# Score bursts of three pieces that run on from batch to batch, in an attention and squared-ReLU kernel

## The chip, the cores and the metric

The kernel runs on one core of one Trainium2 chip. A core has five engines, each with a queue of its own that is worked through in order: TensorE (PE) multiplies matrices into the eight banks of PSUM, VectorE (DVE) and ScalarE (ACT) move and transform data, GpSimd (POOL) does casts here, and SyncE (SP) issues most of the DMA transfers. Instructions wait for each other through semaphores. The metric is the device time of one execution in microseconds, lower is better. The kernel before takes 339.43 us, the median of three runs (338.14 to 339.49).

## The reference

Eight batches of eight heads, 576 tokens, 64 channels per head; 16 beacon keys and values stand ahead of the 576 ordinary ones and are seen by every token. The attention output becomes 4608 rows of 512 channels, which go through a two-layer network with a squared ReLU.

```python
k_all = np.concatenate([beacon_k, k], axis=2)          # (8, 8, 592, 64)
v_all = np.concatenate([beacon_v, v], axis=2)
scores = scale * np.matmul(q, k_all.transpose(0, 1, 3, 2))
scores = np.where(causal, -1e9, scores)                # causal for the 576 keys
a = np.exp(scores - scores.max(-1, keepdims=True))
a /= a.sum(-1, keepdims=True) + 1e-09
x = np.matmul(a, v_all)                                # then to (4608, 512)
h = x @ w_in                                           # (512, 2048)
out = np.square(np.maximum(h, 0)) @ w_out              # (2048, 512)
```

## The kernel before, in words

**Attention.** A batch `b` has four head pairs; pair `p = 4 * b + pr`. Queries and keys are held transposed (`qT`, `kT`: channels of the two heads on partitions 0-63 and 64-127), keys in five blocks of 128. Only the block pairs on or below the diagonal are computed. For batches 1 to 7 the scores of a pair are cut into four *pieces* (`WHOLE`, pieces 0 to 3): three pieces with 512 columns per head, and a fourth with 128 columns (keys of block 0, queries 368 to 496). A piece takes a pair of PSUM banks, one for each head; ScalarE's `exp` (line 781) moves it to its offset in the pair's buffer `pt` (four of these). In the kernel before, the fourth pieces of pairs 0 and 1 share one pair of banks, and those of pairs 2 and 3 another (`SHARED`), each still with an `exp` of its own into its own `pt`. So a batch has 14 bank pairs of scores and 16 `exp`.

**Bursts.** The score matmuls (line 764) use half of the array's rows for each head, the two heads at once; the planner calls this mode "rows", all other matmuls are "full". Scores are issued in *bursts*: one planned operation `qk<pair>.0.<first piece>` computes two or three bank pairs back to back (`SIZES`). From batch 2 on a batch is five bursts of 3, 3, 3, 3 and 2 bank pairs.

**After a pair's four exps** VectorE masks the diagonal (lines 799, 803, `mask`), TensorE multiplies by the values (line 819, `av`: 30 matmuls with `pt` as the weights), and VectorE divides by the sum (lines 834, 835, `norm`) into `xn`. When all four pairs of a batch are normalized, five DMA transposes `xt<b>.0` to `xt<b>.4` (line 866, issued by SyncE, one for each 128-token tile of the batch) put the batch into `xT`, channels on partitions. Batch 0 does this on TensorE instead.

**The network.** The 4608 tokens are worked in nine chunks of 512 (`chunk j`). A chunk has 16 groups `s1.<j>.<f>` of four matmuls (line 947: `xT` by `w_in`), whose results ACT or DVE move with a ReLU (lines 964, 966) and DVE squares (line 973), then 32 blocks of matmuls `s2` (line 987: by `w_out`), whose results ACT copies out (line 437) and SyncE stores, two stores `st<j>.0` and `st<j>.1` for a chunk (line 1012). A chunk begins when its tokens are in `xT`: chunk 3 (tokens 1536 to 2047) needs `xt3.0` to `xt3.2` of batch 3 (which begins at token 1728), chunk 4 (2048 to 2559) needs `xt4.0` to `xt4.2`. Chunk 4 wraps around the ring that `xT` is, so each of its groups is two times four matmuls of 256 columns, and only the second four read batch 4.

**Loads.** `ld<b>k<c>`, `ld<b>q<c>`, `ld<b>v<c>` bring 128 rows of keys, queries or values each into one of eight staging buffers `stg` (lines 483, 484; 256 KB for 128 rows, and a small one of the beacon rows ahead of block 0), GpSimd casts them to bf16 (line 439). From batch 3 on queries and keys are transposed by one large DMA each, `tr<b>q` and `tr<b>k` (line 516), out of `qk_area`. From batch 2 on all of these, the `xt` and the `st` are issued by SyncE, one queue in order.

**What sets the order.** Nothing is scheduled at run time: `Order.run` plans the whole program once, with a duration for each operation, pools for the PSUM banks and buffers, and a list of free engines. On each engine it starts, of the operations whose dependencies, buffers and gate are satisfied in its plan, the one with the lowest `prio`. The order so found is what each engine's queue contains; on the chip the engines follow it, each waiting where data are not there. A burst's `prio` is 100 times its first pair plus the number of its first piece.

Of the kernel before, what the change touches and what calls it, by code (L numbers as in the profile page):

```python
# [129 lines left out]
class Order:  # L130
# [180 lines left out]
def kernel(  # L311
# [11 lines left out]
    nc = tc.nc  # L323
# [17 lines left out]
    def sb(name, shape, dt):  # L341
        return pool.tile(shape, dt, name=name)
# [16 lines left out]
          for i in range(2)]  # L359
    ks = [qk_area[0:NP, (2 * i + 1) * WS:(2 * i + 2) * WS].rearrange("p (h s d) -> p h s d", h=H, s=NS)  # L360
          for i in range(2)]
    bks = sb("bks", [128, H, D], BF16)
    spare = {x: sb(f"spare{x}", [NP, NS * 2 * D], BF16) for x in "kq"}
    vb = [sb(f"vb{i}", [128, NT, H, D + 1], BF16) for i in range(2)]
# [13 lines left out]
    def pair(op, k=0):  # L378
        return ps[:, op.held[k]:op.held[k] + 2, :]
# [4 lines left out]
    def act(n):  # L384
        return 0.066 + n / 1200.0
# [6 lines left out]
    def wait_for(later, first):  # L392
# [1 line left out]
            mybir.DependencyClass.Sync, mybir.DependencyReason.DATA), reason="order of loads")  # L394

    order = Order(
        pools={"ps": Banks(), "stg": Slots(NSTG), "pt": Slots(NPT)},
        limits={"late": 4, "strip": 6, "av": 4, "mlp": 4, "tp": 6},
        floors={"mlp": 2},
        keep=2,  # L400
# [266 lines left out]
    class Phase:  # L667
# [3 lines left out]
        def __init__(self, pieces, diag, last, tiles, off):  # L671
# [30 lines left out]
    ONE_BY_ONE = [[(x, i)] for x in range(HP) for i in range(4)]  # L702
    SHARED = [[(0, 0)], [(0, 1)], [(0, 2)], [(0, 3), (1, 3)], [(1, 0)], [(1, 1)], [(1, 2)], [(2, 0)], [(2, 1)],
              [(2, 2)], [(2, 3), (3, 3)], [(3, 0)], [(3, 1)], [(3, 2)]]
    PIECES = {b: ONE_BY_ONE if b < 1 else SHARED for b in range(B)}
    SIZES = {b: [2] * 7 if b < 2 else [3, 3, 3, 3, 2] for b in range(B)}

    def phases(b):
        return SPLIT if b < NSPLIT else WHOLE
# [26 lines left out]
    def add_scores(pairs, n, sizes, pieces):  # L736

        work = []
        for shared in pieces:
            at, parts = 0, []  # L740
            for x, i in shared:
                parts.append((pairs[x], i, at, phases(pairs[x].b)[n].pieces[i]))
                at += parts[-1][3][2]
            work.append(parts)
        exps = {x.p: [] for x in pairs}
        at = 0
        for size in sizes:
            group = work[at:at + size]
            at += size
            lead = group[0][0][0]  # L750
            prio = 100.0 * lead.p + 1000.0 * n + group[0][0][1]
            every = [part for parts in group for part in parts]
            cols = sum(t1 - t0 for _, _, _, (mms, _, _) in every for _, t0, t1, _ in mms)
            owners = list({x.p: x for x, _, _, _ in every}.values())
            box = {}

            def emit_qk(e, group=group, box=box):
                for k, parts in enumerate(group):
                    st = pair(box["qk"], k)
                    for x, _, lo, (mms, _, _) in parts:  # L760
                        for c, t0, t1, col in mms:
                            for hj in range(2):
                                hp = slice(64 * hj, 64 * hj + 64)
                                nc.tensor.matmul(  # L764
                                    st[:, hj, lo + col:lo + col + t1 - t0],
                                    kT[x.b % 2][hp, x.pr, 128 * c:128 * c + 128],
                                    qT[x.b % 2][hp, x.pr, t0:t1],
                                    start=True, stop=True,
                                )

            qk = add(f"qk{lead.p}.{n}.{group[0][0][1]}", "PE", cols / 2400.0, emit_qk, prio=prio,
                     deps=[d for x in owners for d in x.qk_deps + [x.take_pt]],
                     take=("ps", "late" if lead.b < NSPLIT and n else "strip", [2] * size), gate=lead.gate, mode="rows")
            box["qk"] = qk
            for x in owners:
                qk_ops[x.p].append(qk)
            for k, parts in enumerate(group):
                own = []
                for x, i, lo, (_, off, width) in parts:
                    def emit_exp(e, off=off, width=width, k=k, x=x, lo=lo, box=box):  # L780
                        nc.scalar.activation(pt[x.take_pt.held[0]][:, :, off:off + width],  # L781
                                             pair(box["qk"], k)[:, :, lo:lo + width], AF.Exp, bias=0.0, scale=scale)

                    own.append(add(f"exp{x.p}.{n}.{i}", "ACT", act(2 * width), emit_exp, prio=prio + 0.1 * k,
                                   deps=[qk], give=(qk, k) if len(parts) == 1 else None))
                    exps[x.p].append(own[-1])
                if len(parts) > 1:
                    add(f"share{lead.p}.{n}.{k}", "-", 0.0, None, deps=own, give=(qk, k))
        assert at == len(work)
        for x in pairs:  # L790
            add_phase(x.b, x.pr, x.p, n, phases(x.b)[n], x.take_pt, exps[x.p])

    def add_phase(b, pr, p, n, ph, take_pt, exps):
# [12 lines left out]
        mask = add(f"mask{p}.{n}", "DVE", 0.08 + 0.15 * ph.diag[3] + (0.26 if ph.last else 0.0), emit_mask,  # L806
                   prio=base, deps=exps + [tri_op])
        tl, nt = ph.tiles, len(ph.tiles)

        def emit_av(e):  # L810
            P = pt[take_pt.held[0]]
            a = pair(av)
            for hj in range(2):
                h = 2 * pr + hj
                for t in tl:
                    for c in range(t + 1):
                        rr = rows_of(c)
                        o = ph.off[c, t]
                        nc.tensor.matmul(  # L819
                            a[:, hj, (t - tl[0]) * (D + 1):(t - tl[0] + 1) * (D + 1)],  # L820
                            P[0:rr, hj, o:o + 128],
                            vb[b % 2][0:rr, c, h, :],
                            start=(c == 0), stop=(c == t),
                        )
# [236 lines left out]
    for b in range(B):  # L1061
# [26 lines left out]
        if b < NSPLIT:  # L1088
            for x in pairs:
                for n, ph in enumerate(phases(b)):  # L1090
                    add_scores([x], n, [1] * len(ph.pieces), [[(0, i)] for i in range(len(ph.pieces))])
        else:
            add_scores(pairs, 0, SIZES[b], PIECES[b])
        if b < NXPE:
            add_xt_pe(b)
        else:
            add_xt(b)
        for j in range(NCH):
            if min(((j + 1) * TCH - 1) // S, B - 1) == b:
                late.append(j)  # L1100
        if b >= 1:
            for j in late:
                add_chunk(j)
            late = []

    turns = TURNS.split()
    named = {o.name: o for o in order.ops}
# [35 lines left out]
```

## Time and profile before

| | us |
|---|---|
| median of three runs | 339.43 |
| lowest and highest | 338.14, 339.49 |
| the profiled execution, its own time | 338.65 |
| its span, first to last instruction | 336.9 |
| PE busy in the span | 327.1 |
| ACT busy | 193.6 |
| DVE busy | 160.5 |
| POOL busy | 86.8 |

The profile has a page and views that are asked of the trace. Busy time counts matmuls, weight loads (PEld), vector and scalar operations and casts; DMA-issuing instructions stand under SPq. A row of the *chain of waits* gives start, length and what the chain ran through: TensorE's matmuls of one line, until another line follows. A row of the *timeline* gives start, length, engine, line and operation; for SPq the length is the time that the issuing instruction held the queue. A row of a *line's view* gives shortest, median and longest duration, first and last start, and the time from issue to landing for DMAs. A row of the *windows* gives each engine's busy time in a stretch, the granted TensorE clock, the busy share of the 16 DMA engines and what they moved.

### The profile page before, as it was taken

Reading aid. Unit: us, or ns where it says so; the run is one execution under the profiler, and the core shown is the slowest. Engines: PE = TensorE matmul, PEld = TensorE weight load, DVE = VectorE, ACT = ScalarE, POOL = GpSimd, SP = SyncE. Lnnn points to the kernel's source line nnn. Section 1 sums busy time; section 2 is a strip of 40 time slices with the busy share of each in tenths; the row PEclk is TensorE's granted clock in tenths of the full one; section 3 lists DMA queues with packets and bytes.
Section 4 is the critical chain, followed back from the end, with each engine's and each line's share of the span. In section 5 each row is a group of like instructions: output and inputs, shape, how many; then the busy total and the mean of one; then the engine's idle time right before and its main releaser. Section 6 shows DMA issues by size and latency. Waiting matters only on the chain.

```text
span 336.9 us, 7692 instructions
## 1 busy us (share of the span) xinstructions
PE 327.1 (97%) x3172; PEld 184.2 (55%) x3172; DVE 160.5 (48%) x323; ACT 193.6 (57%) x300; POOL 86.8 (26%) x135
## 2 busy tenths in 40 slices
PE   3999999999999999999999999999999999999995
PEld 2778766545545555554468845545554544444444
DVE  6669977267604761475245632673246503301400
ACT  3887974597457647465656745755656226515611
POOL 7765911425122605140512351220000000000000
PEclk9999999999999999999999999999999999999999
DMA  9999999699959999799989996991310041011003
GB/s 167 196 207 210 206 203 207 147 247 179 221 104 223 241 199 176 185 208 228 206 121 257 242 210 138 209 196 32 104 62 2 14 120 63 0 62 64 0 17 110
DMA packets 138211, 50.38 MB, mean 150 GB/s; under 512 B 124176, under 2 KB 133264, under 8 KB 138176
## 3 DMA queue, kind: packets, MB, share of 16 engines
q1 hardware_dynamic: 128304, 40.42, 57.7%
q0 software_dynamic: 9520, 9.11, 16.3%
q8 instruction: 25, 0.41, 0.6%
q10 hardware_dynamic: 352, 0.36, 0.4%
q14 instruction: 10, 0.08, 0.1%
HBM read 37.22 MB, written 9.44 MB: 138 GB/s over the span
## 4 chain that ended last, share of the span: by engine, by line
PE 93%; DMA 2%; POOL 1%; DVE 1%; issue 1%; ACT 0%; POOLq 0%
PE ps L947 37%; PE ps L987 36%; PE ps L819 9%; PE ps L764 8%; DMA qk_area<-in_q_dram 2%; PE ps L635 1%; PE ps L1030 1%; POOL qk_area L599 1%; PE ps L883 1%; DVE g L966 0%; PE ps L537 0%; POOL vb L439 0%; PE ps L533 0%; POOL w_in L908 0%; DVE g L973 0%
## 5 line engine op out<-in xcount | busy, mean ns | idle before, releaser
L947 PE MATMUL ps<-xT,w_in 128*128 128x512 bf16 (+3 forms) x704 | 133.7, 340 | 0.2
L987 PE MATMUL ps<-w_out,g 128*128 128x512 bf16 x560 | 128.4, 379 | 0.0
L781 ACT ACTIVATE pt<-ps 128x1024 bf16<-128x1024 f32 (+3 forms) x128 | 102.9, 874 | 18.3 <-PE ps L764 18.1
L947 PEld LDWEIGHTS <-w_in 128*128 128x128 bf16 x704 | 65.9, 98 | 55.2 <-issue 3.9
L964 ACT ACTIVATE g<-ps 128x512 bf16<-128x512 f32 (+2 forms) x116 | 65.5, 568 | 39.1 <-PE ps L947 38.6
L987 PEld LDWEIGHTS <-g 128*128 128x128 bf16 x560 | 52.1, 98 | 61.1 <-issue 3.6
L973 DVE TENSOR_TENSOR g<-g 128x1024 bf16<-128x1024 bf16 (+2 forms) x80 | 52.1, 654 | 69.6 <-ACT g L964 69.4
L437 ACT COPY osb<-ps 128x512 f32<-128x512 f32 (+2 forms) x37 | 21.3, 576 | 68.8 <-PE ps L987 54.6
L439 POOL CAST qk_area<-stg 128x512 bf16<-128x512 f32 (+2 forms) x50 | 34.2, 688 | 67.5 <-DMA stg<-in_q_dram 41.0
L439 POOL CAST vb<-stg 128x512 bf16<-128x512 f32 (+1 forms) x39 | 26.1, 675 | 63.3 <-DMA stg<-in_v_dram 63.2
L799 DVE TENSOR_TENSOR pt<-pt,tri 128x1024 bf16<-128x1024 bf16 (+1 forms) x36 | 23.5, 654 | 34.2 <-ACT pt L781 34.2
L819 PEld LDWEIGHTS <-pt 128*128 128x128 bf16 (+1 forms) x960 | 34.2, 98 | 6.3 <-ACT pt L781 0.4
L966 DVE TENSOR_SCALAR g<-ps 128x512 bf16<-128x512 f32 (+2 forms) x44 | 26.8, 611 | 19.7 <-PE ps L947 19.4
L819 PE MATMUL ps<-vb,pt 128*128 128x65 bf16 (+1 forms) x960 | 35.6, 195 | 0.4 <-POOL vb L439 0.3
L764 PE MATMUL ps<-qT,kT 64*128 64x80 bf16 (+6 forms) x680 | 32.9, 235 | 0.0
L764 PEld LDWEIGHTS <-kT 64*128 64x128 bf16 x680 | 19.0, 96 | 16.8 <-issue 13.8
L835 DVE TENSOR_TENSOR xn<-ps,rcp 128x640 bf16<-128x640 f32 (+2 forms) x36 | 27.0, 750 | 1.8 <-DVE rcp L834 0.5
L834 DVE RECIPROCAL rcp<-ps 128x10 f32<-128x10 f32 (+2 forms) x36 | 7.5, 209 | 28.9 <-PE ps L819 28.9
L437 ACT COPY qT<-ps 128x576 bf16<-128x576 bf16 x12 | 7.6, 644 | 8.4 <-PE ps L635 7.4
L803 DVE TENSOR_TENSOR pt<-pt,tri 80x160 bf16<-80x160 bf16 x32 | 11.1, 347 | 0.0
L439 DVE COPY kT<-ps 128x576 bf16<-128x576 bf16 x12 | 8.9, 751 | 1.8 <-PE ps L638 1.2
L635 PE MATMUL ps<-ident,sparek 96*128 96x96 bf16 x18 | 1.5, 229 | 5.8 <-DVE sparek L439 5.8
(52 smaller groups left out, 80.4 us busy)
## 6 DMA issues: line engine op xcount, KB each, us to landing
out_dram<-osb SPq DMA_DIRECT2D x17, 512.0 KB, 3.6
stg<-in_v_dram SPq DMA_DIRECT2D x20, 256.0 KB, 5.1
stg<-in_q_dram SPq DMA_DIRECT2D x20, 256.0 KB, 5.5
stg<-in_k_dram SPq DMA_DIRECT2D x15, 256.0 KB, 4.3
w_in<-in_moe_w_in_dram POOLq DMA_DIRECT2D x4, 512.0 KB, 8.8
w_out<-in_moe_w_out_dram POOLq DMA_DIRECT2D x4, 512.0 KB, 11.6
stg<-in_v_dram SPq DMA_DIRECT2D x7, 224.0 KB, 4.5
qk_area<-in_k_dram POOLq DMA_DIRECT2D x4, 288.0 KB, 11.5
```

The lines of the kernel that those rows point to most:

```text
L437: nc.scalar.copy(dst, src)
L439: eng[e].tensor_copy(dst, src)
L764: nc.tensor.matmul(st[:, hj, lo + col:lo + col + t1 - t0], kT[x.b % 2][hp, x.pr, 128 * c:128 * c + 128], qT[x.b % 2][hp, x.pr, t0:t1], sta ...
L781: nc.scalar.activation(pt[x.take_pt.held[0]][:, :, off:off + width], pair(box["qk"], k)[:, :, lo:lo + width], AF.Exp, bias=0.0, scale=scale)
L799: nc.vector.tensor_tensor(out=d, in0=d, in1=tri[:, m0:m0 + m, :][:, None].to_broadcast([128, 2, m, 128]), op=ALU.min)
L819: nc.tensor.matmul(a[:, hj, (t - tl[0]) * (D + 1):(t - tl[0] + 1) * (D + 1)], P[0:rr, hj, o:o + 128], vb[b % 2][0:rr, c, h, :], start=(c = ...
L835: nc.vector.tensor_tensor(out=xn[b % 2].rearrange("p t (h d) -> p h t d", d=D)[:, 2 * pr:2 * pr + 2, tl[0]:tl[0] + nt], in0=a[:, :, :, 0:D ...
L947: nc.tensor.matmul(h[:, lo - spans[0][0]:hi - spans[0][0]], w_in_sb[:, mc, ft * 128:(ft + 1) * 128], xT[:, mc, lo % RING:lo % RING + hi - lo],
L964: nc.scalar.activation(dst, h, AF.Relu, bias=0.0, scale=1.0)
L966: nc.vector.tensor_scalar(out=dst, in0=h, scalar1=0.0, scalar2=None, op0=ALU.max)
L973: nc.vector.tensor_tensor(out=d, in0=d, in1=d, op=ALU.mult)
L987: nc.tensor.matmul(o, G[:, fc, ts * 128:(ts + 1) * 128], w_out_sb[:, fc, :], start=(fc == 0), stop=(fc == NFT - 1))
```

## The change

For batches 3 to 7 (`FLOW = 3`) the fourth pieces of all four pairs go into one bank pair, 128 columns for each pair, with one `exp` (`expr<b>`) that moves the 1024 columns to a place of its own, `rest` (two buffers, in the part of `qk_area` that the keys of batch 1 used), from which `av` takes the weights for that block. A batch then has 13 bank pairs and 13 `exp`. These form a list, `flow`: the fourth pieces first, then pieces 0, 1, 2 of each pair. Bursts take three from the head of the list, and what is left of a batch waits for the next batch and is issued in one burst with its first pieces; only after batch 7 is a shorter burst made (two). The operations after the scores are added to the plan when a pair's pieces have all been put into bursts. Batches 0 to 2 are unchanged.

```diff
+    rest = [qk_area[:, 4 * W + 1024 * i:4 * W + 1024 * (i + 1)].rearrange("p (h w) -> p h w", h=2) for i in range(2)]
...
-        pools={"ps": Banks(), "stg": Slots(NSTG), "pt": Slots(NPT)},
+        pools={"ps": Banks(), "stg": Slots(NSTG), "pt": Slots(NPT), "rest": Slots(2)},
...
-    PIECES = {b: ONE_BY_ONE if b < 1 else SHARED for b in range(B)}
-    SIZES = {b: [2] * 7 if b < 2 else [3, 3, 3, 3, 2] for b in range(B)}
+    PIECES = {0: ONE_BY_ONE, 1: SHARED, 2: SHARED}
+    SIZES = {0: [2] * 7, 1: [2] * 7, 2: [3, 3, 3, 3, 2]}
+    FLOW = 3
...
+        slots = [x.take_pt for x, _, _, (_, off, _) in every if off is not None] + [
+            x.take_rest for x, _, _, (_, off, _) in every if off is None]
...
+            if parts[0][3][1] is None:
+                x = parts[0][0]
+
+                def emit_rest(e, k=k, x=x, box=box):
+                    nc.scalar.activation(rest[x.take_rest.held[0]], pair(box["qk"], k), AF.Exp, bias=0.0, scale=scale)
+
+                o = add(f"expr{x.b}", "ACT", act(2 * 512), emit_rest, prio=prio + 0.1 * k, deps=[qk], give=(qk, k))
+                for x, _, _, _ in parts:
+                    exps[x.p].append(o)
+                continue
...
+    def add_flow(pairs, last):
...
+        pieces = WHOLE[0].pieces
+        (c, t0, t1, _), = pieces[3][0]
+        flow.append([(x, 3, 128 * n, ([(c, t0, t1, 0)], None, 128)) for n, x in enumerate(pairs)])
+        flow.extend([(x, i, 0, pieces[i])] for x in pairs for i in range(3))
+        done = []
+        while len(flow) >= 3 or (last and flow):
+            group = [flow.pop(0) for _ in range(min(3, len(flow)))]
+            add_burst(group, 0, flow_exps)
+            for parts in group:
+                for x, _, _, _ in parts:
+                    flow_left[x.p] -= 1
+                    if not flow_left[x.p]:
+                        add_phase(x.b, x.pr, x.p, 0, phases(x.b)[0], x.take_pt, flow_exps[x.p], x)
+                        if x.pr == HP - 1:
+                            add(f"restg{x.b}", "-", 0.0, None, deps=[o for i in range(HP) for o in av_ops[HP * x.b + i]],
+                                give=x.take_rest)
+                            done.append(x.b)
+        return done
...
                         o = ph.off[c, t]
+                        keys = P[0:rr, hj, o:o + 128]
+                        if x is not None and (c, t) == (0, 3):
+                            keys = rest[x.take_rest.held[0]][:, hj, 128 * pr:128 * pr + 128]
...
-        else:
+        elif b < FLOW:
             add_scores(pairs, 0, SIZES[b], PIECES[b])
...
+        for bb in add_flow(pairs, b == B - 1) if b >= FLOW else [b]:
+            if bb < NXPE:
+                add_xt_pe(bb)
+            else:
+                add_xt(bb)
```

The bodies of the bursts moved from `add_scores` into `add_burst` are otherwise as before.

More of the change, by code (lines that the diff above doesn't have):

```diff
@@ L747, in add_scores @@
         for size in sizes:
-            group = work[at:at + size]
+            add_burst(work[at:at + size], n, exps)
             at += size
[L750 to L788, printed above, removed]
@@ L791, in add_scores, with add_burst, emit_qk, emit_exp @@
             add_phase(x.b, x.pr, x.p, n, phases(x.b)[n], x.take_pt, exps[x.p])
-    def add_phase(b, pr, p, n, ph, take_pt, exps):
+    def add_burst(group, n, exps):
+        lead = group[0][0][0]
+        prio = 100.0 * lead.p + 1000.0 * n + group[0][0][1]
+        every = [part for parts in group for part in parts]
+        cols = sum(t1 - t0 for _, _, _, (mms, _, _) in every for _, t0, t1, _ in mms)
+        owners = list({x.p: x for x, _, _, _ in every}.values())
+        slots = [x.take_pt for x, _, _, (_, off, _) in every if off is not None] + [
+            x.take_rest for x, _, _, (_, off, _) in every if off is None]
+        box = {}
+        def emit_qk(e, group=group, box=box):
+            for k, parts in enumerate(group):
+                st = pair(box["qk"], k)
+                for x, _, lo, (mms, _, _) in parts:
+                    for c, t0, t1, col in mms:
+                        for hj in range(2):
+                            hp = slice(64 * hj, 64 * hj + 64)
+                            nc.tensor.matmul(
+                                st[:, hj, lo + col:lo + col + t1 - t0],
+                                kT[x.b % 2][hp, x.pr, 128 * c:128 * c + 128],
+                                qT[x.b % 2][hp, x.pr, t0:t1],
+                                start=True, stop=True,
+                            )
+        qk = add(f"qk{lead.p}.{n}.{group[0][0][1]}", "PE", cols / 2400.0, emit_qk, prio=prio,
+                 deps=[d for x in owners for d in x.qk_deps] + list({id(o): o for o in slots}.values()),
+                 take=("ps", "late" if lead.b < NSPLIT and n else "strip", [2] * len(group)), gate=lead.gate, mode="rows")
+        box["qk"] = qk
+        for x in owners:
+            qk_ops[x.p].append(qk)
+        for k, parts in enumerate(group):
+            own = []
+            if parts[0][3][1] is None:
[6 more added lines that the diff above has]
+                continue
+            for x, i, lo, (_, off, width) in parts:
+                def emit_exp(e, off=off, width=width, k=k, x=x, lo=lo, box=box):
+                    nc.scalar.activation(pt[x.take_pt.held[0]][:, :, off:off + width],
+                                         pair(box["qk"], k)[:, :, lo:lo + width], AF.Exp, bias=0.0, scale=scale)
+                own.append(add(f"exp{x.p}.{n}.{i}", "ACT", act(2 * width), emit_exp, prio=prio + 0.1 * k,
+                               deps=[qk], give=(qk, k) if len(parts) == 1 else None))
+                exps[x.p].append(own[-1])
+            if len(parts) > 1:
+                add(f"share{lead.p}.{n}.{k}", "-", 0.0, None, deps=own, give=(qk, k))
@@ new lines @@
+    flow, flow_exps, flow_left, whole = [], {}, {}, []
+    def add_flow(pairs, last):
+        b = pairs[0].b
+        take_rest = add(f"rest{b}", "-", 0.0, None, prio=100.0 * pairs[0].p, deps=pairs[0].qk_deps, take=("rest", "rest", [1]),
+                        gate=pairs[0].gate)
+        for x in pairs:
+            x.take_rest = take_rest
+            flow_exps[x.p] = []
+            flow_left[x.p] = 4
+        pieces = WHOLE[0].pieces
[16 more added lines that the diff above has]
+        return done
@@ L794, in add_phase @@
+    def add_phase(b, pr, p, n, ph, take_pt, exps, x=None):
         base = 100.0 * p + 1000.0 * n
@@ L818, in emit_av @@
                         o = ph.off[c, t]
+                        keys = P[0:rr, hj, o:o + 128]
+                        if x is not None and (c, t) == (0, 3):
+                            keys = rest[x.take_rest.held[0]][:, hj, 128 * pr:128 * pr + 128]
                         nc.tensor.matmul(
                             a[:, hj, (t - tl[0]) * (D + 1):(t - tl[0] + 1) * (D + 1)],
-                            P[0:rr, hj, o:o + 128],
+                            keys,
                             vb[b % 2][0:rr, c, h, :],
@@ L1091 @@
                     add_scores([x], n, [1] * len(ph.pieces), [[(0, i)] for i in range(len(ph.pieces))])
-        else:
+        elif b < FLOW:
             add_scores(pairs, 0, SIZES[b], PIECES[b])
[L1094 to L1104, printed above, removed]
+        for bb in add_flow(pairs, b == B - 1) if b >= FLOW else [b]:
[3 more added lines that the diff above has]
+                add_xt(bb)
+            for j in range(NCH):
+                if min(((j + 1) * TCH - 1) // S, B - 1) == bb:
+                    late.append(j)
+            if bb >= 1:
+                for j in late:
+                    add_chunk(j)
+                late = []
     turns = TURNS.split()
```

## The prediction

> **What bounds the kernel now.** I read the page's busy shares first, then the windows, to see where the busiest engine has gaps, then the chain of waits.
>
> ```profile
> PE 327.1 (97%) x3172; PEld 184.2 (55%) x3172; DVE 160.5 (48%) x323; ACT 193.6 (57%) x300; POOL 86.8 (26%) x135
> ```
>
> ```profile
> 0.00:66.25 66.25, 59.78 (x837) 42.88 (x838) 47.95 (x131) 44.51 (x74) 36.78 (x61) 1.00 1.08 192
> 66.25:333.54 267.29, 267.28 (x2336) 141.32 (x2336) 112.30 (x191) 148.82 (x226) 50.05 (x74) 1.00 0.68 140
> 333.54:336.90 3.36, 0.00 (x0) 0.00 (x0) 0.29 (x1) 0.27 (x1) 0.00 (x0) 1.00 0.27 88
> ```
>
> In a row of the windows the first number after the stretch is its length, the second TensorE's busy time, and the last three are the granted clock, the DMA share and GB/s. From 66.25 to 333.54 us TensorE has no gap: 267.28 of 267.29 us, at clock 1.00. The idle time lies ahead of that, in a part the change does not touch. So two things alone can move the time: work taken off TensorE counts in full, and so does each new wait of TensorE, since its queue is in order and nothing behind a waiting matmul can pass it.
>
> **What the change takes away: three bursts.** What a burst costs beside its columns is read from the chain of waits.
>
> ```profile
> 160.18 1.73 PE ps L987 x8
> 161.91 0.77 PE ps L764 x20
> 162.68 3.56 PE ps L987 x16
> 166.24 0.67 PE ps L764 x20
> 166.91 1.83 PE ps L987 x8
> ...
> 224.10 0.54 PE ps L764 x8
> ...
> 232.58 0.77 PE ps L764 x20
> ```
>
> Eight `s2` matmuls of 512 columns take 1.73 us after a value burst, so 0.216 each or 0.422 ns a column, and 1.83 us right after a score burst: leaving a burst costs 0.10. The bursts of 0.77, 0.67 and 0.54 us have 1536, 1280 and 1024 columns for each of two heads that run at once; at 0.422 ns that is 0.65, 0.54 and 0.43, so entering costs 0.11 to 0.13. I take 0.2 us for a burst in all. Five batches had 25 bursts; five times 13 bank pairs in threes are 21 bursts and one of two, 22. Columns and matmuls stay the same in number. Gain: 3 x 0.2 = 0.6 us. A bound from the other side is the time that the weight loader stood idle:
>
> ```profile
> PEld L764 <- issue: 13.8, 37, 0.4
> ...
> PEld L987 <- issue: 3.6, 17, 0.2
> ```
>
> 13.8 over 37 entries is 0.37 and 3.6 over 17 exits is 0.21; if all of it were lost array time, a burst would cost 0.58 and the gain be 1.7 us. The straight line through the three lengths (0.23 us for 512 columns leaves 0.08 at none) gives 0.18 a burst, 0.5 us. I take 0.6, because the lengths of whole matmul runs are closer to what the end sees than the idle time of a loader that runs ahead.
>
> **What it changes off the path.** A batch loses four exps of 256 elements and gets one of 1024:
>
> ```profile
> L781 ACT ACTIVATE pt<-ps 128x1024 bf16<-128x1024 f32 x84 | 82.7, 1034 | 8.3 <-PE ps L764 8.3
> ...
> L781 ACT ACTIVATE pt<-ps 128x256 bf16<-128x256 f32 x28 | 9.5, 395 | 8.5 <-PE ps L764 8.5
> ```
>
> 4 x 0.395 - 1.034 = 0.55 us less for ScalarE in each batch, 2.7 in all. ScalarE is 57% busy and its idle time costs nothing, so I count 0; between 0 and the 2.7 us gain that would follow if TensorE waited for it, the window without a gap says 0. If that cover went, by an exp that came late, TensorE would wait about one exp, 1.03 us. The value matmuls load the same 128x128 weights from `rest` instead of `pt`: no change. In batches 3 and 6 the burst that begins with the fourth pieces is planned behind the one that begins with the first pair's piece 2 (its number, 3, is the higher), which delays `av12` by one burst, with other work in between.
>
> **What it moves: the DMA transposes behind loads.** The two programs' orders, which are fixed when they are built, differ on two queues. On TensorE a batch's last pair is finished later, since its last piece waits for the next batch: of batch 3, `av15` now comes after four runs of eight `s2` matmuls of chunk 2 rather than after one. Behind it the planner has put more of SyncE's loads ahead of the transposes that feed the network. Ahead of `xt3.0` now stand in addition `ld5q3`, `ld5k1`, `ld5q4`, `ld5k2` and the store `st2.0`; ahead of `xt4.0` in addition `ld6q4`, `ld6k2`, `ld6k3`, `ld6k4` and `ld6v0`. The matmuls that read these transposes keep about their place on TensorE. So the question is what room the transposes have.
>
> ```profile
> 126.18 3.51 SPq L484 DMA_DIRECT2D stg<-in_q_dram  x3
> 129.79 7.72 SPq L866 DMA_TRANSPOSE xT<-xn  x5
> ...
> 137.60 0.53 SPq L484 DMA_DIRECT2D stg<-in_q_dram  x1
> 138.23 0.53 SPq L484 DMA_DIRECT2D stg<-in_k_dram  x1
> 138.85 0.95 SPq L1012 DMA_DIRECT2D out_dram<-osb  x1
> 139.89 0.65 SPq L484 DMA_DIRECT2D stg<-in_q_dram  x1
> 140.64 0.86 SPq L484 DMA_DIRECT2D stg<-in_k_dram  x1
> ```
>
> ```profile
> L866 SPq DMA_TRANSPOSE xT<-xn x2: 1260/1616/1973, 131.6 to 133.6; - x2
> ...
> DMA to landing us min/median/max: 2.6/3.3/4.1
> ```
>
> ```profile
> L866 SPq DMA_TRANSPOSE xT<-xn x2: 1257/1257/1257, 167.3 to 168.6; - x2
> ...
> DMA to landing us min/median/max: 2.6/3.4/4.2
> ```
>
> The first fence is SyncE's queue: the five rows after the transposes are just the five instructions that now go ahead of them. The other two hold `xt3.1` and `xt3.2`, and `xt4.1` and `xt4.2`: of the first two, the second (issued at 133.6) landed 2.6 us later, at 136.2; of the others, the second (168.6) took 4.2 and landed at 172.8. When are they wanted?
>
> ```profile
> 138.74 0.86 PE ps L947 x4
> ...
> 173.99 0.87 PE ps L947 x8
> ```
>
> Those are the first groups of chunks 3 and 4: the transposes had 2.5 and 1.6 us to spare (chunk 4 reads batch 4 only with its second four matmuls, at 174.4). In the changed order, ahead of chunk 3 stand one `s2` run of eight more (+1.73), one burst fewer (-0.2) and 256 columns fewer (-0.11): it is reached at 140.15. Ahead of chunk 4: +1.73, two bursts fewer (-0.4), 768 columns fewer (-0.32): 175.0, its second half at 175.4.
>
> How late do the transposes become? Cheapest, as the five moved instructions went in the trace with an emptied queue: 137.60 to 141.50, 3.9 us. Dearest, where the queue is full:
>
> ```profile
> 159.35 5.23 SPq L484 DMA_DIRECT2D stg<-in_q_dram  x4
> ...
> 173.06 0.63 SPq L484 DMA_DIRECT2D stg<-in_q_dram  x1
> ...
> 175.07 0.72 SPq L1012 DMA_DIRECT2D out_dram<-osb  x1
> 175.89 0.42 SPq L484 DMA_DIRECT2D stg<-in_k_dram  x1
> ...
> 178.12 3.78 SPq L516 DMA_TRANSPOSE qT<-qk_area  x1
> ...
> 197.78 0.77 SPq L484 DMA_DIRECT2D stg<-in_q_dram  x1
> ...
> 217.59 2.34 SPq L1012 DMA_DIRECT2D out_dram<-osb  x1
> ```
>
> There a load holds SyncE 1.31 us (5.23 / 4) and a store 2.34: 4 x 1.31 + 2.34 = 7.6. The queue is full at the place: the three loads ahead of 129.79 took 1.2 each. I take three loads at 1.31, the half-size `ld5q4` at 0.77 (197.78) and the store at 0.95, 5.7 us. `xt3.2` lands at 136.2 + 5.7 = 141.9, wanted at 140.15: TensorE waits 1.75. For batch 4, cheapest, 173.06 to 178.12 without the store (0.82 to the next issue), 4.2; dearest 5 x 1.31 + 0.7 for the beacon rows, 7.2; I take the middle, 5.7. `xt4.2` lands at 178.5, wanted at 175.4: 3.1. That is counted against the order without waits, so the 1.75 is part of it: 1.75 at chunk 3, 1.35 more at chunk 4, 3.1 together (1.6 to 4.6 by the bounds). Behind the waiting `s1` stand all of TensorE's later work, then the ReLUs and exps that follow it; no engine can make it up, as the window shows no later gap to fall into. Batches 5 to 7 keep more room: SyncE has gone through the same transfers in both orders by then, apart from `ld7k3`.
>
> Sum: 338.65 (the profiled execution) - 0.6 + 3.1 = 341.15. This execution stands 0.8 under the median of the three runs shown; on the median the same is 341.9. I predict 341.4, between the two.
>
> **Rivals.** *The transposes come in time* (the other side). For it:
>
> ```profile
> 130.00:136.00 6.00, 6.00 (x71) 3.12 (x69) 2.30 (x4) 3.05 (x6) 2.77 (x4) 1.00 1.02 153
> 136.00:142.00 6.00, 6.00 (x71) 3.42 (x71) 2.58 (x5) 3.34 (x4) 0.62 (x1) 1.00 0.72 169
> ```
>
> The DMA engines had 28% of 6 us, 1.7 us, free behind the transposes, and loads put there cost 0.53. If the push of the queue is absorbed there, so that `xt4.2` is at most 2.6 us later, no wait is left at chunk 4: 338.65 - 0.6 = 338.05, 338.8 on the median. Against it: share 1.02 just where the loads go in.
>
> *The keys of batch 7 decide.* The burst that runs from batch 6 into 7 needs `tr7k` 7.5 us ahead of the place it had (232.58, now about 225.1: 224.10 plus one `s1` group, 512 columns and less two bursts, plus its first piece).
>
> ```profile
> L516 SPq DMA_TRANSPOSE kT<-qk_area x1: 4503/4503/4503, 220.0 to 220.0; - x1
> ...
> DMA to landing us min/median/max: 5.9/5.9/5.9
> ```
>
> It landed at 225.9. Alone this would be a wait of 0.8, hidden in the 3.1 above, since the same transfers stand ahead of it in both orders. If the 5.7 were still there at 220, it would be 6.5: 338.65 - 0.6 + 6.5 = 344.5.
>
> *A slower clock after the wait.* If a wait of some 2 us made the clock fall, the four groups behind it (16 matmuls, 3.5 us) would take twice as long: 341.15 + 3.5 = 344.6. Against it: clock 1.00 over the first 66 us, with 6.5 us of gaps. The Trainium skill, "TensorE: Matmul & The Clock Gate", Part 1, says that the clock drops to half after an idle window of about 3.4 us; by that rule waits of 1.75 and 1.35 would not do it, one of 4 could; no row here shows such a drop.
>
> **Chances.** Forecast 0.62 (338.65 - 0.6 + 1.6 to 4.6, so 339.7 to 342.7); in time 0.28; keys of batch 7 0.06; clock 0.04. A difference under 0.5% (1.7 us) is about what a measurement of this kernel cannot tell from none. Slower by more needs waits over 2.3 us: 0.50 of the forecast's 0.62, and the last two cases, 0.60. Faster by more needs no wait and a burst worth 0.58: 0.06. The rest, 0.34, is within. The range goes from the in-time case, 338.2, to the forecast's upper bound on the median, 343.4.
>
> **What would show it.** Right: 22 bursts of line 764's successor from batch 3 on; TensorE idle just ahead of the first `s1` group of chunks 3 and 4, released by a DMA into `xT`, 1 to 3 us each; SyncE's `xt3.0` near 135.5 and `xt4.0` near 171.3; after that no gap. Wrong: no such idle time (the transposes have room), idle time ahead of a score burst released by `kT` (the second rival), or by exps (my zero for ScalarE); granted clock under 1.00.

## The result, and the profile after

| | median, us | lowest to highest, runs | ratio to the kernel before, 95% interval |
|---|---|---|---|
| before, in the same session | 338.62 | 336.95 to 341.79, 12 | |
| changed | 340.67 | 338.79 to 342.11, 12 | 1.0048 [1.0025, 1.0071] |

The ratio comes from rounds in which both kernels ran, and is worth 338.62 x 0.0048 = 1.6 us. Here and below a ratio leaves out the runs that showed a lower granted clock and a longer time (two of `dose`), while medians and ranges take in all. The changed kernel is slower, by an amount at the edge of the 0.5% that the prediction called measurable: the interval leaves out 1 and takes in 1.005. The predicted time, 341.4, is 0.7 us too high. The profiled execution took 340.68, 2.03 more than the profiled one of before.

The page's busy times, and the window from 66.25 to 336.00 us, which ends 0.43 us behind the last matmul (after the length: PE, PEld, DVE, ACT, POOL busy; then clock, DMA share, GB/s), both of the changed kernel:

```profile
PE 326.8 (96%) x3172; PEld 185.0 (55%) x3172; DVE 160.8 (47%) x319; ACT 196.4 (58%) x289; POOL 87.0 (26%) x135
```

```profile
66.25:336.00 269.75, 268.33 (x2359) 142.83 (x2357) 111.47 (x188) 152.74 (x218) 50.23 (x74) 1.00 0.69 139
```

ScalarE's busy time did not fall by 2.7, as the prediction had it, but rose from 193.6 to 196.4; among other things it was given four more ReLUs of 512 columns (101 instead of 97), which VectorE did before. TensorE was idle for 0.01 us of its part without gaps before; now 269.75 - 268.33 = 1.42, of which 0.43 lies behind the last matmul (333.81 + 1.76 = 335.57) and 0.99 is waiting. The view of the waits says for what (sum, times, longest, in us), and the chain of waits shows it in order:

```profile
PEld L777 <- DMA kT<-qk_area: 1.3, 1, 1.3
...
PE ps L777 <- DMA kT<-qk_area: 1.0, 1, 1.0
```

```profile
94.53 0.77 PE ps L777 x20
...
141.56 3.56 PE ps L1000 x16
...
176.47 2.62 PE ps L1000 x24
...
218.43 0.36 PE ps L777 x5
218.79 8.73 DMA kT<-qk_area
...
227.57 0.62 PE ps L777 x20
...
333.81 1.76 PE ps L1083 x16
```

Line 777 is the score matmul of the changed kernel (764 before), line 1000 is `s1` (947), line 1083 the closing `s2` (1030). A row with DMA begins where the transfer was issued, not where TensorE began to wait for it. The one wait is that of the burst which runs from batch 6 into batch 7, for the large transpose of the keys, `tr7k`. At chunk 3 (141.56) and chunk 4 (176.47), where the prediction put 3.1 us of waiting, the chain has no transfer. Yet the loads had gone ahead of the transposes as it said; SyncE's queue:

```profile
126.29 4.37 SPq L485 DMA_DIRECT2D stg<-in_q_dram  x4
130.75 1.05 SPq L485 DMA_DIRECT2D stg<-in_k_dram  x1
131.90 1.29 SPq L485 DMA_DIRECT2D stg<-in_q_dram  x1
133.28 0.57 SPq L485 DMA_DIRECT2D stg<-in_k_dram  x1
133.95 1.02 SPq L1065 DMA_DIRECT2D out_dram<-osb  x1
135.06 7.28 SPq L919 DMA_TRANSPOSE xT<-xn  x5
```

`xt3.0` was issued at 135.06, 8.77 us after the first of the loads of queries (126.29); before it was 3.61 after it (126.18 to 129.79). The two transposes that the chunks wait for, `xt3.2` and `xt4.2`, are the last ones of these two answers on line 919:

```profile
L919 SPq DMA_TRANSPOSE xT<-xn x2: 1257/1257/1257, 137.2 to 138.5; - x2
...
DMA to landing us min/median/max: 2.7/3.1/3.6
```

```profile
L919 SPq DMA_TRANSPOSE xT<-xn x2: 1252/1256/1260, 171.5 to 172.8; - x2
...
DMA to landing us min/median/max: 2.5/2.9/3.2
```

Each of the two has the shortest landing of its pair: 138.5 + 2.7 = 141.2, only 0.4 ahead of 141.56, and 172.8 + 2.5 = 175.3, 1.2 ahead of 176.47 (and 0.4 more ahead of the second four matmuls of chunk 4, which alone read batch 4).

**A measure that is finer than the total.** The first score burst of batch 3 starts at 94.53 here and at 93.13 in the trace of before, though the two programs are the same up to it. What the change does lies between this burst and the end of the last matmul, and this *stretch* can be read from the first and the last row of any chain above: 333.81 + 1.76 - 94.53 = 241.04, against 331.78 + 1.76 - 93.13 = 240.41. The changed work took 0.63 us longer, and the other 1.4 of the 2.03 lay ahead of it. The rows of before:

```profile
93.13 0.77 PE ps L764 x20
...
331.78 1.76 PE ps L1030 x16
```

### The profile page after: what moved, and what is told of

Read it like the earlier page. It is cut to its first block, busy times and chain, and to the rows that moved or that the text cites. A ratio compares the mean times of both kernels' runs of the same rounds, so it can differ in the third digit from the quotient of the medians.

```text
span 339.0 us, 7646 instructions
## 1 busy us (share of the span) xinstructions
PE 326.8 (96%) x3172; PEld 185.0 (55%) x3172; DVE 160.8 (47%) x319; ACT 196.4 (58%) x289; POOL 87.0 (26%) x135
## 4 chain that ended last, share of the span: by engine, by line
PE 93%; DMA 4%; DVE 2%; issue 0%; ACT 0%
PE ps L1040 36%; PE ps L1000 35%; PE ps L872 9%; PE ps L777 8%; DMA kT<-qk_area 3%; PE ps L636 1%; DMA g<-in_k_dram 1%; PE ps L1083 1%; PE ps L639 1%; PE ps L936 1%; DVE g L1019 1%; DVE g L1026 0%; DVE qk_area L440 0%; PE ps L538 0%; ACT pt L804 0%
## 5 line engine op out<-in xcount | busy, mean ns | idle before, releaser
L804 ACT ACTIVATE pt<-ps 128x1024 bf16<-128x1024 f32 (+4 forms) x108 | 97.9, 961 | 16.4 <-PE ps L777 16.3
L1017 ACT ACTIVATE g<-ps 128x512 bf16<-128x512 f32 (+2 forms) x120 | 67.7, 567 | 40.8 <-PE ps L1000 40.0
L1026 DVE TENSOR_TENSOR g<-g 128x1024 bf16<-128x1024 bf16 (+2 forms) x80 | 53.7, 673 | 62.2 <-ACT g L1017 61.2
L440 POOL CAST vb<-stg 128x512 bf16<-128x512 f32 (+1 forms) x39 | 26.8, 696 | 63.4 <-DMA stg<-in_v_dram 44.4
L1019 DVE TENSOR_SCALAR g<-ps 128x512 bf16<-128x512 f32 (+2 forms) x40 | 24.1, 602 | 22.7 <-PE ps L1000 22.4
L872 PE MATMUL ps<-vb,qk_area 128*128 128x65 bf16 x40 | 7.8, 194 | 0.0
```

Of the source, the lines that this page charges most:

```text
L440: eng[e].tensor_copy(dst, src)
L872: nc.tensor.matmul(a[:, hj, (t - tl[0]) * (D + 1):(t - tl[0] + 1) * (D + 1)], keys, vb[b % 2][0:rr, c, h, :], start=(c == 0), stop=(c == t),)
L1017: nc.scalar.activation(dst, h, AF.Relu, bias=0.0, scale=1.0)
L1019: nc.vector.tensor_scalar(out=dst, in0=h, scalar1=0.0, scalar2=None, op0=ALU.max)
L1026: nc.vector.tensor_tensor(out=d, in0=d, in1=d, op=ALU.mult)
```

## The experiments

Three theories stood at the start. **X**: waits of chunks 3 and 4 for `xT`, as predicted, which come in most executions though not in the profiled one. **K**: the keys of batch 7 alone. **S**: the later start belongs to the change. All stretches are worked out as above, from the rows of the first burst and of the last closing matmuls; the waits are those of TensorE's matmuls (PE rows) in the view of the waits.

| profiled execution | start | stretch | waits, us |
|---|---|---|---|
| before | 93.13 | 240.41 | none |
| before_again | 91.59 | 240.61 | none |
| before3 | 94.47 | 240.93 | VectorE 0.4 |
| changed | 94.53 | 241.04 | kT 1.0 |
| again (changed) | 92.21 | 241.30 | xT 0.4, kT 0.9 |
| again2 (changed) | 92.74 | 242.99 | xT 2.1 in two, kT 0.6 |
| flush6 | 93.69 | 240.13 | none |
| keys7 | 93.53 | 240.25 | xT 0.4 |
| xtfirst | 92.48 | 239.76 | none |
| xtfirst2 | 92.69 | 240.05 | none |
| flushall | 92.97 | 240.39 | none |
| seven | 92.98 | 242.52 | none |
| dose | 94.03 | 243.93 | xT 2.4 in two, kT 1.4 |

The three executions of the kernel before lie 0.5 us apart, which is how fine this measure is for one trace; most of it is the wait of 0.4 for VectorE in before3.

**again, again2, before_again, before3: both kernels unchanged, once more.**

> The changed kernel once more. Theory K (the keys of batch 7 set the end: the burst that runs from batch 6 into 7 waits for their DMA, which goes by the DMA queue and not by TensorE's pace): 340 to 341.5 us, TensorE idle ahead of that burst by 1.3 us when it reaches chunk 2's place as late as in the profile shown (first score burst of batch 3 at 94.5) and by 2.5 to 3 when it is there at 93.1, the keys landing at 226 to 229 either way. Theory X (the transposes into xT are late): idle at the first s1 of chunks 3 and 4, 1 us or more when the first score burst of batch 3 is at 93.1. Theory S (the 1.4 us at the start belong to the changed program): the first score burst of batch 3 at 94.5 again.

> The kernel before once more, for where its first score burst of batch 3 stands and what lies behind it. Theory K and X alike: the start moves from execution to execution, here between 92 and 94.6 us, and behind it 240.4 us to the end of the last matmul, as in the profile shown (333.54 - 93.13), whatever the start. Theory S: 93.1 again, within 0.2.

> The changed kernel a third time. 239.7 us of TensorE work behind the first score burst of batch 3, and waits of 1.0 to 1.7 us in all at chunk 3 and ahead of the burst that needs the keys of batch 7: 240.8 to 241.5 for that stretch, ratio 1.003 to 1.005.

> The kernel before a third time: 240.4 to 240.6 us behind its first score burst of batch 3, wherever that stands between 91.5 and 94.6.

The chain of before_again:

```profile
91.59 0.77 PE ps L764 x20
...
330.44 1.76 PE ps L1030 x16
```

The repeats of the changed kernel took 339.65 us (ratio 1.004 [1.0024, 1.0056], 6 runs) and 340.83 (ratio 1.0035 [1.0002, 1.0068], 12 runs); the kernel before took 337.31 and 340.61 in one run each. The starts of the changed kernel are 94.53, 92.21 and 92.74, those of before 93.13, 91.59 and 94.47: they overlap, so S falls. The stretches do not: 241.04 to 242.99 against 240.41 to 240.93. Their means are 241.78 and 240.65, 1.13 apart. Not all went as expected: before3 came above its 240.4 to 240.6, by that wait for VectorE, and again2's 242.99 is above its 240.8 to 241.5. K as `again` had it, with keys that land by the pace of the DMA queue alone and a wait of 2.5 to 3 us after an early start, missed as well: with the start at 92.21 the wait was 0.9. The waits and the chain of again2 show where its time went:

```profile
PE ps L1000 <- DMA xT<-xn: 2.1, 2, 1.5
...
PE ps L777 <- DMA kT<-qk_area: 0.6, 1, 0.6
```

```profile
92.74 0.77 PE ps L777 x20
...
172.70 4.48 DMA xT<-xn
...
177.31 2.34 PE ps L1000 x20
...
219.78 7.89 DMA kT<-qk_area
...
333.97 1.76 PE ps L1083 x16
```

This execution has waits of the kind that was predicted: 0.6 at chunk 3 and 1.5 at chunk 4, where `xt4.2`, issued at 172.70, took 4.48 us to land. In the profile shown first the same transpose was issued at 172.8 and took 2.5. From the start that is 172.70 - 92.74 = 80.0 and 172.8 - 94.53 = 78.3: issued 1.7 later and landed 2.0 slower, so the same program has the wait at chunk 4 in one execution and 1.2 us to spare in another. The wait for the keys is there in all three traces.

The DMA view of these two flights, from issue to landing, tells them apart (queue, packets, MB, share of the 16 engines); first the changed kernel's first profile, 172.78 to 175.27, then again2, 172.70 to 177.18:

```profile
q1 hardware_dynamic: 1605, 0.38, 95.6%
```

```profile
q1 hardware_dynamic: 1632, 0.40, 63.6%
q8 instruction: 1, 0.02, 1.9%
```

While `xt4.2` was under way in again2, one 16 KB packet of the queue that the profile calls `q8 instruction` was moved too; in the first profile the next such packet began 0.9 us after `xt4.2` had landed. In the thirteen profiles `xt4.2` took 4.1 to 4.5 us in the four in which such a packet began during its flight (before, before_again, again2, dose) and 2.5 in the other nine. No run moved the packet, so that it causes the delay is not shown by an experiment, though the two go together without exception. The 4.2 us on which the prediction built was such a flight.

**keys7: only `tr7k` is put ahead of the values of batch 7.** The line makes the planner hold `ld7v1` back until `tr7k` is issued.

```diff
     named["ld1v0"].behind.append(named["cast0v4"])
+    named["ld7v1"].behind.append(named["tr7k"])
```

> On SyncE the loads of batch 7's values, blocks 1 to 4, stand behind the transpose of its keys. TensorE's order is that of the changed kernel up to batch 6. Theory K: the keys land some 2 us earlier, near 225, and the wait shrinks to below 1 us: 338.4 to 339.6; the values come later, and the value burst of pair 28 could wait for them. Theory X: unchanged, 340.3 to 341.

338.68 us (336.59 to 339.2, 12 runs), ratio 1.0005 [0.9989, 1.002]. The view of line 517, first of the changed kernel, then of keys7 (issue, then time to landing), and the waits of keys7:

```profile
L517 SPq DMA_TRANSPOSE kT<-qk_area x1: 5734/5734/5734, 218.8 to 218.8; - x1
...
DMA to landing us min/median/max: 8.7/8.7/8.7
```

```profile
L517 SPq DMA_TRANSPOSE kT<-qk_area x1: 3634/3634/3634, 217.7 to 217.7; - x1
...
DMA to landing us min/median/max: 5.6/5.6/5.6
```

```profile
PEld L1000 <- DMA xT<-xn: 0.6, 1, 0.6
...
PE ps L1000 <- DMA xT<-xn: 0.4, 1, 0.4
```

Without three of the four value loads ahead of it the transpose lands 5.6 us after its issue rather than 8.7, the wait for the keys is gone, and the wait at chunk 3 stays. The time is inside what K expected and below X's 340.3. The edit also moves a store, and TensorE's order of the other work around batch 7; up to there both orders are those of the changed kernel. Against `again` of the same session (1.004) the ratio fell by 0.0035, or 1.2 us, and the waits for the keys that went were 0.6 to 1.0 in the traces. By this run about 1 us of the changed kernel's loss is the keys of batch 7; the runs of flush6, next, do not agree.

**flush6: the run-on from batch 6 to 7 is left out, so batch 6 ends with a burst of its own (23 bursts).**

```diff
-        for bb in add_flow(pairs, b == B - 1) if b >= FLOW else [b]:
+        for bb in add_flow(pairs, b in (6, B - 1)) if b >= FLOW else [b]:
```

> No burst runs from batch 6 into 7: 23 bursts, and the keys of batch 7 are first needed 8 us later. Theory K: no wait for them, so the gain of two bursts, 0.4 us, is all that is left: 338 to 338.6 where the kernel before takes 338.6. Theory X: as the changed kernel, 340.3 to 341, since the order up to batch 6 is the same. Theory S: 339.6 to 340.

339.25 us (338.65 to 341.32, 12 runs), ratio 1.0034 [1.0017, 1.0051]: a miss for K, which had 338 to 338.6. The profile has no wait for `kT`, as K says, and a short stretch of 240.13. SyncE's order is that of the changed kernel. So the profiled execution gained what K expects and the runs together did not. That would fit waits at chunks 3 and 4 in other executions, as between the changed kernel's own traces, but the trace of this kernel does not show them, and keys7, which would have the same waits, came to 1.0005 in the same session: inconclusive.

**xtfirst, xtfirst2: the transposes of batches 3 and 4 go ahead of the loads again.**

```diff
     named["ld1v0"].behind.append(named["cast0v4"])
+    named["ld5q3"].behind.append(named["xt3.4"])
+    named["ld6q4"].behind.append(named["xt4.4"])
```

> On SyncE the transposes of batches 3 and 4 stand ahead of the loads again that the change put ahead of them (ld5q3 and what follows, ld6q4 and what follows). TensorE's order is that of the changed kernel. Theory X: no wait at chunks 3 and 4, 338 to 338.8. Theory K: the wait for the keys of batch 7 stays or grows, since SyncE waits for batch 3 and the later loads begin later: 340.5 to 342.5.

> The transposes of batches 3 and 4 ahead of the loads again, a second time, with more rounds. Both waits are gone, so 22 bursts in place of 25 are all that is left: 0.6 to 0.7 us under the kernel before, ratio 0.9975 to 0.9985.

337.48 us (337.17 to 340.17, 8 runs), ratio 0.998 [0.9955, 1.0005]; the repeat 337.99 (337.07 to 341.19, 12 runs), ratio 0.998 [0.9952, 1.0008]. SyncE's queue, the chain and line 517 of xtfirst:

```profile
129.63 0.38 SPq L1065 DMA_DIRECT2D out_dram<-osb  x1
131.06 7.21 SPq L919 DMA_TRANSPOSE xT<-xn  x5
138.38 0.53 SPq L485 DMA_DIRECT2D stg<-in_q_dram  x1
```

```profile
92.48 0.77 PE ps L777 x20
...
330.48 1.76 PE ps L1083 x16
```

```profile
L517 SPq DMA_TRANSPOSE kT<-qk_area x1: 4941/4941/4941, 215.7 to 215.7; - x1
...
DMA to landing us min/median/max: 7.0/7.0/7.0
```

No wait for `xT` or `kT` is left in either trace, and the stretch is 239.76, and 240.05 in xtfirst2: that is TensorE's work with 22 bursts and no transfer in its way, 0.65 and 0.36 less than the 240.41 with 25. But two lines move more than they name. TensorE's order is not quite that of the changed kernel: the eighth burst begins 50.4 us after the start rather than 53.2 to 53.9. Behind the transposes the planner also issued `tr7k` ahead of the values of batch 7, at 215.7, and it landed in time. So this run takes out X and K at once and does not tell one from the other; K's expectation of 340.5 to 342.5 missed for this reason. It is the fastest version: by the ratios of one session (1.004 for `again`, 0.998) 0.6% faster than the changed kernel. It is also 0.2% below the kernel before in two sessions, but each of the two intervals takes in 1, so that gain is seen in the stretches and not shown by the times.

**dose: the push of SyncE is enlarged.** Ahead of `xt3.0` SyncE issues two more loads of 147 KB each into memory that is free by then.

```diff
                 at = tok % RING
+                if b == 3 and t == 0:
+                    for y in "kq":
+                        nc.sync.dma_start(out=spare[y].bitcast(FP32).rearrange("p (h d) -> p h d", d=D),
+                                          in_=q[5, 0:6, 384:480, :].transpose([1, 0, 2]))
```

> The changed kernel with two loads more on SyncE just ahead of xt3.0 (147 KB each, into buffers that nothing reads any more); TensorE's order unchanged. Theory X: chunk 3 waits 1.0 to 1.5 us longer, about 1.5 to 2 in all, and if SyncE has made up for the two loads when the keys of batch 7 are transposed, the wait for those is shorter by as much as TensorE came later: 340 to 340.6 in all, else up to 341.5. Theory K alone: no wait at chunk 3, time as the changed kernel.

341.7 us (339.15 to 345.84, 10 runs), ratio 1.0056 [1.0027, 1.0085], worth 338.92 x 0.0056 = 1.9 us. So the ratio puts it at 340.8, inside the 340 to 341.5 that X expected; the median of all ten is 0.2 above. K alone, with no wait at chunk 3, fell. The waits and the chain of dose (line 1004 is `s1` here):

```profile
PE ps L1004 <- DMA xT<-xn: 2.4, 2, 1.3
...
PE ps L777 <- DMA kT<-qk_area: 1.4, 1, 1.4
```

```profile
94.03 0.77 PE ps L777 x20
...
174.42 4.20 DMA xT<-xn
...
221.06 8.84 DMA kT<-qk_area
...
336.20 1.76 PE ps L1087 x16
```

Two loads more give waits of 1.3 at chunk 3 and 1.1 at chunk 4, the latter with the slow kind of flight of `xt4.2` (4.20): the mechanism of the prediction works where the transposes have no room left. The lateness was not made up by batch 4 or by batch 7, where the wait for the keys did not shrink but was 1.4. The stretch of 243.93 is 2.9 longer than that of the changed kernel's first profile.

**seven: the kernel before with smaller bursts, seven of two bank pairs in every batch but batch 2 (35 instead of 25 from batch 3 on).**

```diff
-    SIZES = {b: [2] * 7 if b < 2 else [3, 3, 3, 3, 2] for b in range(B)}
+    SIZES = {b: [2] * 7 if b != 2 else [3, 3, 3, 3, 2] for b in range(B)}
```

> The kernel before, with seven bursts of two bank pairs for a batch from batch 3 on, 35 in place of 25; columns and exps the same. At 0.2 us a burst TensorE has 2.0 us more: from the first score burst of batch 3 to the last matmul's end 242.4 us instead of 240.4, ratio 1.005 to 1.007. At the weight loader's 0.58: 246.2, ratio 1.017. If a burst costs nothing: 240.4.

340.76 us (339.83 to 342.23, 10 runs), ratio 1.0055 [1.0031, 1.0079], worth 338.92 x 0.0055 = 1.9 us. The chain:

```profile
92.98 0.55 PE ps L764 x16
...
333.74 1.76 PE ps L1030 x16
```

The stretch is 242.52, with no wait for a transfer, 2.1 above the 240.41 with 25 bursts (1.9 above 240.61): 0.2 us for each of ten bursts. That is the price that the prediction took, and the 242.4 that was expected.

**flushall: the fourth pieces are merged, but nothing runs on (bursts of 3, 3, 3, 3 and 1, 25 in all).**

```diff
-        for bb in add_flow(pairs, b == B - 1) if b >= FLOW else [b]:
+        for bb in add_flow(pairs, True) if b >= FLOW else [b]:
```

> The fourth pieces of four pairs in one with its own place, but no burst runs from batch to batch: bursts of 3, 3, 3, 3 and 1, 25 as before. SyncE's order is nearly that of the kernel before. Theory X with K: no wait and no gain, 240.3 to 240.6 us from the first score burst of batch 3 to the last matmul's end, ratio 0.999 to 1.001. If merging the fourth pieces itself cost or gained: off that by what it does, a gain of up to 2.7 us if ScalarE's saved time counted.

338.66 us (337.99 to 342.03, 12 runs), ratio 1.0003 [0.9978, 1.0027]; its chain:

```profile
92.97 0.77 PE ps L777 x20
...
331.60 1.76 PE ps L1083 x16
```

The stretch is 240.39 against 240.41 before, with no wait for a transfer. One `exp` of 1024 columns instead of four of 256 is worth nothing that can be seen (the plan gave ScalarE nine more ReLUs of 512 columns, 106 instead of 97), and the new place of the fourth pieces costs nothing either. Gain and loss of the change both come from the run-on.

## Why the prediction was partly right

- **TensorE decides, and each new wait counts in full: right.** The matmul waits for `xT` and `kT` in the three traces of the changed kernel are 1.0, 1.3 and 2.7. Without them the stretches are 240.0, 240.0 and 240.3, close to the 239.76 and 240.05 of the two xtfirst traces, which have no such wait.
- **A burst at 0.2 us, a gain of 0.6: right, if a little high.** Ten more bursts cost 2.1. Less their waits, the stretches of the six traces with 22 bursts (three of the changed kernel, keys7, two of xtfirst) are 240.0 on the mean, from 239.8 to 240.3, and those of the three with 25 are 240.5, from 240.4 to 240.6: three bursts saved 0.5. The bound from the idle weight loader (1.7 us) was far off, so its idle time was not lost time of the array.
- **ScalarE's saving at 0: right** by flushall, though the saving itself did not come: ScalarE's busy time rose from 193.6 to 196.4.
- **The push of the transposes, 5.7 us: right in kind, somewhat too large.** Relative to the start, `xt3.0` is issued at 36.66, 35.74 and 35.38 in the three traces of before and at 40.53, 41.15 and 41.44 in those of the changed kernel: 5.1 later on the mean. `xt4.0` is at 72.50, 72.16 and 71.10, and at 75.61, 76.59 and 77.35: 4.6 later. The moved loads took nearly what was forecast, since in the queue `xt3.0` stands 8.77 behind the first load of queries rather than 3.61, which is 5.2.
- **The waits, 1.75 at chunk 3 and 1.35 more at chunk 4: the step that failed.** Measured: 0, 0.4 and 0.6 at chunk 3, and 0, 0 and 1.5 at chunk 4. The demand was right: `xt3.2` was wanted at 140.15 - 93.13 = 47.0 from the start, and chunk 3 did begin at 141.56 - 94.53 = 47.0. The supply was put 1.7 too late: forecast was `xt3.2` at 141.9 - 93.13 = 48.8, and it came at 46.6, 47.2 and 47.5, on the mean 47.1. In the three traces of before it had landed at 43.0, 42.6 and 42.6, on the mean 42.7. So its landing moved by 4.4 and not by 5.7, which is 1.3 of the 1.7, and the other 0.3 is that the sum started from the latest of the three. For `xt4.2` the forecast was 178.5 - 93.13 = 85.4; it came at 80.7, 81.7 and 84.4. The sum took over the 4.2 us of landing of the one execution that it knew, a flight with the 16 KB packet in it; in the changed kernel it was 2.5 in two traces and 4.5 in again2, and the 2 us between them are more than the whole wait.
- **The keys of batch 7, "hidden in the 3.1": the second step that failed.** Taken alone its 0.8 was nearly right. `tr7k` landed at 227.52 - 94.53 = 133.0 from the start, before at 225.9 - 93.13 = 132.8: the same landing, though it was issued 2.6 earlier (218.79 - 94.53 = 124.3 against 220.03 - 93.13 = 126.9). The wait was 0.6 to 1.0 in all three traces. It was not hidden, for two reasons: there was less ahead of it, and where the chunks waited (2.1 in again2) the keys came later as well, at 219.78 + 7.89 - 92.74 = 134.9 (and in dose, with 2.4 of such waits, at 135.9). The forecast had moved the demand and left the supply in place, but the loads behind which the keys stand are held back with TensorE.
- **A slower clock after the wait: not seen.** The granted clock of the window with the 1 us wait is 1.00, and so it is over the stretch of again2, with a wait of 1.5. The rule of the Trainium skill, "TensorE: Matmul & The Clock Gate", Part 1, that it takes an idle window of some 3.4 us, agrees with that; no wait here is that long. Behind the last matmul the granted clock did fall to 0.50, in flush6 already 2.0 us after it and in before_again after 5.2.

The sum came near the result with its parts interchanged: it had 3.1 us of waits for `xT` and none for the keys, less 0.6, so +2.5; the three traces show 1.7 of waits on the mean, half of it for the keys (0.8), less 0.5 for the bursts, so +1.2, where their stretches show +1.1; the runs show +1.6, with both inside their interval (0.85 to 2.4). That the number came out so near was in part luck: a wait that was forecast too large stood in for one that was forecast as hidden. The in-time rival described chunks 3 and 4 of the first trace better than the forecast did, but missed the keys.

Two things stay open: whether the 16 KB packet itself slows `xt4.2` or only comes with what does, and why flush6's runs did not gain what keys7's did.

## What to carry to other kernels

Where an in-order engine has no gap, a change that saves time on it must also be followed through the queue that feeds it: here the run-on that saved about 0.5 us of array time also reordered the DMA issues. Transposes that had 2.5 and 1.6 us to spare in the trace of before, and keys that had 6.7 (232.58 - 225.9), came up to 1.5 us late. A margin of that size cannot be judged from one execution; take the supply and the demand of several, relative to a point that both kernels share, and measure the changed stretch inside the trace rather than the total. Two ordering constraints, transposes ahead of loads that nobody waits for yet, kept the shorter stretch without the waits, in both traces of xtfirst.

## What the runs showed of the hardware

- The start of the same early program moves between executions: the first burst of batch 3 begins between 91.59 and 94.53 us in the thirteen profiles above, at a granted clock of 1.00, and totals follow it. The cause was not looked for.
- A large transpose takes by what is queued ahead of it: `tr7k` landed 5.6 us after its issue when one value load and a store stood just ahead, 8.7 behind three more value loads. Issuing it earlier behind the same transfers did not make it land earlier: 126.9 us after the start or 124.3, it landed at 132.8 and 133.0.
- One small transpose of the same program (`xt4.2`) landed 2.5 us after its issue in one execution and 4.5 in another; over thirteen profiles the long flights (4.1 to 4.5) are those during which a 16 KB packet of `q8 instruction` began.
- A load of 256 KB held SyncE for 1.09 us on the mean of four (4.37 / 4), and one load held it 0.53 right behind five transposes (138.38 in xtfirst).
